# Attention with a pooled query, then a gated feed-forward: gates that take two heads on 128 partitions, a row tile per head into one PSUM bank

## The chip, the cores and the metric

The kernel runs on one core of a Trainium2 chip. The metric is device time in microseconds (us) of the whole kernel. Next to the time stands one profiled execution, whose trace gives every instruction's start, duration and what ended the engine's idle time. The kernel works in fp16 and fp32 and needs fp32 rows at the end.

## The reference, cut to what matters

Eight batches of eight heads, 1152 positions, 64 elements a head. Queries are averaged in pairs (576 rows), attend to 1152 keys, and the heads side by side (4608 rows of 512) go through a product of two gates and two more matrices.

```python
def _attn_ref(q, k, v):
    q_pool = q.reshape(B, H, S // 2, 2, D).mean(axis=3)
    scores = scale * np.matmul(q_pool, k.transpose(0, 1, 3, 2))
    attn = np.exp(scores - np.max(scores, axis=-1, keepdims=True))
    attn = attn / (np.sum(attn, axis=-1, keepdims=True) + 1e-09)
    return np.matmul(attn, v)

def _moe_ref(x, w1, w2, w3, w_out):      # x: 4608 x 512, dff = 1024
    a = x @ w1
    b = x @ w2
    h = a * b @ w3
    return h @ w_out
```

## The kernel before, in words

**Attention.** Work goes by pairs of heads: 32 pairs P, four to a batch. A head has 64 elements, so TensorE is used as two row tiles of 64 partitions that work beside each other; tile u holds head u of the pair. `scores` (L316) forms blocks of 512 columns of both heads into one of two double banks `psc`, and one exponential on ScalarE (`expo`, L322) of 128x1024 follows each: 324 of them, 10.125 a pair. They go into a ring `er`. When a pair's scores are through, `attend` (L339, L348) multiplies the probabilities with the values, 36 products of 65 columns for each head and 18 for the last 64 query rows of both; these products use the full array. `normalize` divides by the row sums on VectorE (L377 to L391) into `xn`, and a DMA on SyncE's queue transposes it to `xT` (L385). The last 64 query rows of each head of a batch (rems) are collected for four batches.

**Feed-forward.** w3 and w_out are multiplied once into T16 (`w3_transpose`, tiles w3t and pT, L513 to L538), so that what is left per batch is: gates `pg` (L580), a = x w1 and b = x w2, their product `gT` on VectorE (L571, after a copy `asb` of a, L558, or L555 on ScalarE after the last scores), and rows `pp` (L612) with T16, scaled into `osb` (L598, L602) and stored by SyncE. Before, `xn` of one head at a time is transposed, so even 128-row chunks of queries lie on partitions 0 to 63 and odd ones on 64 to 127: row tile 0 takes 256 tokens, row tile 1 the 256 others, over eight heads. Each tile fills a bank of its own with a and b (2 x 256 columns), with 16 products. Tile 1 needs the weights of every head on partitions 64 to 127 too and tile 0 on 0 to 63; so `swap_halves` (L445 to L452) makes a second copy of w1 and w2 with the halves swapped: 16 full-array products with a permutation, and 12 VectorE and 4 ScalarE copies. `cross` (L406) does the same for the remainders with DMAs.

**Two tiles in one bank.** Rows and T16 products sum over both tiles into one bank. There tile 0 does its eight products, VectorE reads an element of the bank (`handed`, L491), and only then does tile 1 add its eight.

**The order.** The schedule is by hand. A loop over the exponentials (L796 to L861) keeps a clock for each row tile, an estimate of VectorE's and ScalarE's progress, and four spare banks (`spare`, `take`, `give`). Scores come as soon as the exponential two before is estimated done (`due`); probability products come at the places in BEHIND and APART (J: both heads together; a digit: so many exponentials apart); in between, `step` emits the next product from two queues of feed-forward work, one for each tile, if its inputs and a bank are estimated ready. Tile 0 may lead tile 1 by LEAD. `add_batch` puts a batch's gates and rows into the queues. After the last exponential (`tail`) two more banks are given to them and ScalarE takes the copies of a and the scaling. The constants T_..., COLD, LANDS, STAGE, PREP, early and V_COPIED are that planner's.

**Loads.** GpSimd issues the loads of keys, queries, values and weights in the order of ORDER; from pair 7 on keys and queries are transposed by DMAs on SyncE's queue (L173, L180), before that by TensorE (`prep_pe`, tile t). The first queries are loaded to 64 partitions and added in pairs by VectorE (L233), transposed by TensorE (tq) and copied (L242).

Of the kernel before, what the change touches and what calls it, by code (L numbers as in the profile page):

```python
# [15 lines left out]
NJ = 9  # L16
# [8 lines left out]
def kernel(  # L25
# [21 lines left out]
    T_SC, T_ACT, T_EXP, T_SEM, T_PV, LEAD = 0.225, 0.93, 1.05, 0.25, (1.78, 1.4), 3.79  # L47
    COLD = 9.0
# [9 lines left out]
    xT = const.tile([128, H, 2, 512], FP16)  # L58
    w1sb = const.tile([128, 2, NC, dff], FP16)
    w2sb = const.tile([128, 2, NC, dff], FP16)  # L60
    T16 = const.tile([128, NF, dm], FP16)
    wosb = const.tile([128, NF, dm], FP16)
    xR0 = const.tile([128, 3, H // 2, 2, 2, 64], FP16)
    xR = [xR0, wosb.rearrange("p a b -> p (a b)")[:, 0:48 * D].rearrange(
        "p (o c k u r) -> p o c k u r", o=3, c=H // 2, k=2, u=2)]
# [3 lines left out]

    ident = const.tile([128, 128], FP16)  # L70
    swap = const.tile([128, 128], FP16)
    seen = const.tile([1, 2], FP16)
    handed = const.tile([1, 1], FP32)
# [69 lines left out]
    def pool_q(P, eng=None):  # L143

        pp, o = P // 2, 64 * (P % 2)
        if P % 2 == 0:
            qps[pp] = ab.tile([128, NJ, 2, D], FP16, tag="qp", bufs=2, name="qp")
        r = slice(o, o + 64)
        src = qst[pp][r].rearrange("p u (c two) d -> p u c two d", two=2)
        (eng or nc.vector).tensor_tensor(  # L150
            out=qps[pp][r].rearrange("p c u d -> p u c d"),
            in0=src[:, :, :, 0, :], in1=src[:, :, :, 1, :], op=ALU.add)
# [67 lines left out]
    def prep_first():  # L220
# [3 lines left out]
        qp = qps[0] = ab.tile([128, NJ, 2, D], FP16, tag="qp", bufs=2, name="qp")  # L224
        src = q0.rearrange("p u (c two) d -> p u c two d", two=2)
# [5 lines left out]
        for cs in parts:  # L231
            r = slice(cs[0], cs[-1] + 1)
            nc.vector.tensor_tensor(  # L233
                out=qp[0:64, r].rearrange("p c u d -> p u c d"),
                in0=src[:, :, r, 0, :], in1=src[:, :, r, 1, :], op=ALU.add)
        for h, cs in enumerate(parts):
            for c in cs:
                o = 64 * (c - cs[0])
                nc.tensor.transpose(tq[:, h, o:o + 64],
                                    qp[0:64, c].rearrange("p u d -> p (u d)"),  # L240
                                    ident[0:64, 0:64])
# [85 lines left out]
    def attend(P, us, js=range(NJ)):  # L327
# [35 lines left out]
        if 0 in us and b % 2 == 1:  # L363
            nc.sync.dma_start_transpose(
                out=xR[b // 4][:, 1, hp, (b // 2) % 2].rearrange("p u r -> p (u r)"),
                in_=rems[:, hp].rearrange("p s d -> p (s d)"))
        if 0 in us and hp == 3:
            landed = vec + (8.0 if b < 2 else 6.5)
            ended.append((b, [landed]))
            if b % 2 == 1:  # L370
                crossing.append((b, landed + (6.0 if b % 4 == 1 else 0.0)))

    def normalize(P, u, po, n, at):
# [5 lines left out]
        xn = ab.tile([128, 4, D], FP16, tag="xn", bufs=4, name="xn")  # L379
        nc.vector.tensor_tensor(  # L380
            out=xn, in0=acc[:, 0:4, 0:D],
            in1=rz[:, 0:4].to_broadcast([128, 4, D]), op=ALU.mult)
        k = (b // 2) % 2
        o = 256 * (b % 2)
        nc.sync.dma_start_transpose(  # L385
            out=xT[:, 2 * hp + u, k, o:o + 256].rearrange("p (i r) -> p i r", r=128),
            in_=xn.rearrange("p i d -> p (i d)"))
        vector(5, at)
        vector(256, at)
        if n == 5:  # L390
            nc.vector.tensor_tensor(  # L391
                out=rems[:, hp, b % 2, :], in0=acc[:, 4, 0:D],
                in1=rz[:, 4].to_broadcast([128, D]), op=ALU.mult)
            vector(64, at)
        return vec

    ended, kq_done, crossing = [], {}, []
    crossed = [[1e9], [1e9]]

    def cross():  # L400

        b, _ = crossing.pop(0)
        x = xR[b // 4]
        k = (b // 2) % 2
        for h in range(2):
            nc.sync.dma_start(out=x[64 * h:64 * h + 64, 2 - 2 * h, :, k],  # L406
                              in_=x[64 - 64 * h:128 - 64 * h, 1, :, k])
        if k == 1:
            crossed[b // 4][0] = max(clock) + 6.0
# [12 lines left out]
    def load_part(h, dst, src):  # L422
        cols = slice(512 * h, 512 * h + 512)
        nc.gpsimd.dma_start(out=dst[:, 0, :, cols],
                            in_=src.rearrange("(c p) f -> p c f", p=128)[:, :, cols])
        swaps[h].extend((dst, c, cols) for c in range(NC))
# [6 lines left out]

    swaps = ([], [])
    copied = [[1e9], [1e9]]

    def swap_halves():

        half = 0 if swaps[0] else 1
        dst, c, cols = swaps[half].pop(0)
        n = take()
        t = bank("sw", n)
        nc.tensor.matmul(t, swap, dst[:, 0, c, cols], start=True, stop=True)  # L445
        clock[:] = [max(clock) + 0.22] * 2
        if c % 3 == 1:
            nc.scalar.copy(out=dst[:, 1, c, cols], in_=t)
            done = exp_done[-1] = max(exp_done[-1], clock[0] + T_SEM) + 0.6
        else:  # L450
            nc.vector.tensor_copy(out=dst[:, 1, c, cols], in_=t)
            done = vector(512, clock[0])  # L452
        give(n, done)
        if not swaps[half]:
            copied[half][0] = done + T_SEM

    def swap_due():
        half = 0 if swaps[0] else 1
        free = 3 if prep[0] or prep[1] else 2
        if not swaps[half]:  # L460
            return False
        landed = LANDS[("f" if swaps[half][0][0] is w1sb else "g") + str(half)] + T_SEM
        return max(clock) > max(WEIGHTS[half], landed) and len(spare) >= free and (
            spare[0][0] < min(clock))
# [3 lines left out]
    class Block:  # L468
# [3 lines left out]
        def __init__(self, pre, n_products, tiles, then, dt=FP32):  # L472
            self.pre, self.n_products, self.tiles, self.then = pre, n_products, tiles, then
            self.dt, self.n, self.handed = dt, None, 1e9

# [5 lines left out]
        def product(self, n, h, emit):  # L481
# [3 lines left out]
            end = n == self.n_products - 1  # L485
# [4 lines left out]
            elif end:  # L490
                nc.vector.tensor_copy(out=handed, in_=self.t[0:1, 0:1])  # L491
                self.handed = vector(1, clock[h]) + T_SEM
# [5 lines left out]
    def add(queue, block, cost, ready, emit):  # L498


        for h in block.tiles:
            for n in range(block.n_products):
                queue[h].append((block, n, cost, ready(n) if callable(ready) else ready, emit))

    def w3_transpose(c):
# [4 lines left out]
        landed = LANDS["wo"]  # L510

        def out(t, at, h):
# [4 lines left out]
            if left[0] == 0:  # L517
                ready[0] = max(done + T_SEM, landed)
# [21 lines left out]
        add(ffn, Block("pT", NF, (0, 1), copy), 0.216, [ready], product)  # L540

    def unit(x, places, ready, split=False, final=False):

        gT = {}
        gdone = [[[1e9] for _ in range(NF)] for _ in range(2)]
        n = 256

        def gate(ft, h, both=False):  # L550
            def mul(t, at):
                asb = ffp.tile([128, n], FP32, tag="asb", bufs=3, name="asb")
                b, a = t[:, n:2 * n], asb
                if tail:
                    nc.scalar.copy(out=a, in_=t[:, 0:n])  # L555
                    at += 0.4
                else:
                    nc.vector.tensor_copy(out=a, in_=t[:, 0:n])  # L558
                    vector(n, at)
                if h not in gT:  # L560
                    if split:
                        g = ffp.tile([128, NF, 128], FP16, tag="row", bufs=7, name="gT")
                        gT[h] = g.rearrange("p a f -> p (a f)").rearrange(
                            "p (a f) -> p a f", f=n)
                    else:
                        gT[h] = ffp.tile([128, NF, n], FP16, tag="g", bufs=4, name="gT")
                g = gT[h][:, ft % 4 if split else ft, 0:n]
                if not split:
# [4 lines left out]
                gdone[h][ft][0] = done + T_SEM  # L573
                return done
            fs = slice(ft * 128, ft * 128 + 128)

            def emit(t, s, i, start, stop):
                w, m = divmod(i, H)
                o = s.start // 64
                nc.tensor.matmul(t[:, n * w:n * w + n], (w1sb, w2sb)[w][s, (m + o) % 2, m // 2, fs],  # L580
                                 x(o, s, m),
                                 start=start, stop=stop, skip_group_check=True)
            if both:
                queue = [], []
                add(queue, Block("pg", H, (0, 1), mul), 0.0025 + n / 2400,
                    [ready, copied[2 * ft // NF]],
                    lambda t, s, i, start, stop: emit(t, s, i + H * (s.start > 0), start, stop))
                for q, add_ in zip(ffn, queue):
                    q[-NF:-NF] = add_
                return  # L590
            add(ffn, Block("pg", 2 * H, (h,), mul), 0.0025 + n / 2400,
                [ready, copied[2 * ft // NF]], emit)

        def rows(h, o, places):
# [11 lines left out]
            cs = slice(o, o + 128)  # L606

            def g(s, i):
                return gT[i // 4][s, i % 4, cs] if split else gT[h][s, i, cs]
# [4 lines left out]
            if final:  # L614
                last.append((emit, store, places, lambda i: g(slice(0, 128), i)))
            else:
                add(ffn, Block("pp", NF, (0, 1), store), 0.216,
                    lambda i: [gdone[i // 4 if split else h][i]], emit)

        yield gate  # L620
        for h, o, to in places:
            rows(h, o, to)

    def add_batch(b, ready):

        k, o, end = (b // 2) % 2, 256 * (b % 2), b == B - 1
# [272 lines left out]
```

## Time and profile before

| what | value |
|---|---|
| runs | 413.22, 416.35, 416.85 us; median 416.35 |
| the profiled execution: own time, span of the trace | 410.37 us, 408.6 us |
| granted TensorE clock, mean | 0.996 |
| instructions in the span | 16883 |
| first scores, first gate | 8.97 us, 72.0 us |
| last product of TensorE ends | 404.7 us |
| LDWEIGHTS with w1 and w2 | 2 x 1152, mean 94 ns |
| transposes xT<-xn on SyncE's queue | 64, median 5.4 us to landing, about 1.2 us to issue |

The profile page gives busy time by engine, a picture in 40 slices, the chain of work that ended last, the costliest groups of instructions (line, engine, operation, tiles, shapes, count, busy us, mean ns, idle time before and what ended it) and DMA issues. A busy TensorE is not one at its peak: its products are pipelined, a 512-column product of a row tile has a duration of 376 ns and the next one on that tile starts sooner. So prices of products are read from their starts. PE is TensorE, PEld its weight loads, DVE VectorE, ACT ScalarE, POOL GpSimd, SP SyncE.

### The profile page before, as it was taken

Reading aid. Unit: us, or ns where it says so; the run is one execution under the profiler, and the core shown is the slowest. Engines: PE = TensorE matmul, PEld = TensorE weight load, DVE = VectorE, ACT = ScalarE, POOL = GpSimd, SP = SyncE. Lnnn points to the kernel's source line nnn. Section 1 sums busy time; section 2 is a strip of 40 time slices with the busy share of each in tenths; the row PEclk is TensorE's granted clock in tenths of the full one; section 3 lists DMA queues with packets and bytes.
Section 4 is the critical chain, followed back from the end, with each engine's and each line's share of the span. In section 5 each row is a group of like instructions: output and inputs, shape, how many; then the busy total and the mean of one; then the engine's idle time right before and its main releaser. Section 6 shows DMA issues by size and latency. Waiting matters only on the chain.

```text
span 408.6 us, 16883 instructions
## 1 busy us (share of the span) xinstructions
PE 392.5 (96%) x7356; PEld 316.5 (77%) x7356; DVE 213.8 (52%) x570; ACT 323.8 (79%) x369; POOL 241.1 (59%) x283
## 2 busy tenths in 40 slices
PE   2799999999999999999999999999999999999996
PEld 1377666868878977897789886799778878998884
DVE  2436775566445644664456654367346644652431
ACT  2979988889889798889988799789889788834432
POOL 6244246596987878779959787687978611000000
PEclk9989999999999999999999999999999999999999
DMA  8999999999999999999999999999999933103004
GB/s 181 210 206 203 177 194 192 147 146 143 165 187 205 126 128 171 189 159 161 192 183 158 131 146 131 189 204 173 118 211 206 118 81 116 29 18 117 3 28 129
DMA packets 121834, 60.99 MB, mean 149 GB/s; under 512 B 71456, under 2 KB 114976, under 8 KB 121760
## 3 DMA queue, kind: packets, MB, share of 16 engines
q0 software_dynamic: 47552, 32.98, 65.7%
q1 hardware_dynamic: 73776, 26.61, 43.2%
q8 instruction: 57, 0.93, 1.0%
q10 hardware_dynamic: 432, 0.33, 0.3%
q14 instruction: 17, 0.14, 0.1%
HBM read 67.11 MB, written 9.44 MB: 187 GB/s over the span
## 4 chain that ended last, share of the span: by engine, by line
PE 90%; DMA 6%; ACT 1%; DVE 1%; issue 1%; SPq 0%
PE pg L580 30%; PE psc L316 19%; PE po L339 18%; PE pp L612 15%; DMA qT<-qp 4%; PE pT L538 3%; PE po L348 3%; ACT er L322 1%; DMA er<-in_q_dram 1%; PE sw L445 1%; PE t L284 1%; PE w3t L522 1%; PE pp L689 0%; DVE w3T L513 0%; DVE kT L278 0%
## 5 line engine op out<-in xcount | busy, mean ns | idle before, releaser
L322 ACT ACTIVATE er<-psc 128x1024 f16<-128x1024 f32 x324 | 303.5, 1046 | 46.5 <-PE psc L316 46.2
L316 PE MATMUL psc<-qT,kT 64*128 64x512 f16 (+7 forms) x1152 | 130.8, 289 | 4.0 <-ACT er L322 3.1
L580 PE MATMUL pg<-xT,w2sb 64*128 64x256 f16 x1024 | 124.5, 269 | 0.8 <-issue 0.8
L580 PE MATMUL pg<-xT,w1sb 64*128 64x256 f16 x1024 | 123.3, 269 | 0.0
L580 PEld LDWEIGHTS <-w2sb 64*128 64x128 f16 x1152 | 93.6, 94 | 8.0 <-issue 1.4
L580 PEld LDWEIGHTS <-w1sb 64*128 64x128 f16 x1152 | 93.1, 94 | 7.7
L612 PE MATMUL pp<-T,gT 64*128 64x512 f16 (+1 forms) x552 | 93.9, 376 | 0.0
L316 PEld LDWEIGHTS <-kT 64*128 64x128 f16 x1152 | 63.8, 95 | 29.0 <-issue 14.1
L339 PEld LDWEIGHTS <-er 128*128 128x128 f16 x2304 | 73.8, 98 | 11.2 <-issue 9.7
L339 PE MATMUL po<-vt,er 128*128 128x65 f16 x2304 | 80.0, 194 | 0.1
L571 DVE TENSOR_TENSOR gT<-pg,asb 128x256 f16<-128x256 f32 x144 | 64.1, 445 | 20.0 <-ACT asb L555 15.0
L558 DVE COPY asb<-pg 128x256 f32<-128x256 f32 x116 | 49.0, 422 | 33.0 <-PE pg L580 32.2
L150 POOL TENSOR_TENSOR qp<-qst 64x1152 f16<-64x1152 f16 x25 | 59.3, 2373 | 2.0 <-DMA qst<-in_q_dram 1.2
L377 DVE RECIPROCAL rz<-po 128x4 f32<-128x4 f32 x64 | 12.1, 189 | 78.8 <-PE po L348 40.9
L612 PEld LDWEIGHTS <-gT 64*128 64x128 f16 (+1 forms) x552 | 39.3, 94 | 13.1 <-issue 0.4
L112 POOL DMA_DIRECT2D kst<-in_k_dram x46 | 33.0, 718 | 4.5 <-issue 4.1
L112 POOL DMA_DIRECT2D vst<-in_v_dram x46 | 33.6, 734 | 0.0
L159 POOL COPY vt<-vst 128x1152 f16<-128x1152 f16 x28 | 32.2, 1154 | 0.6
L185 POOL COPY seen<-kT 1x1 f16<-1x1 f16 x24 | 4.3, 179 | 47.5 <-DMA kT<-kc 47.5
L165 POOL COPY kc<-kst 128x1152 f16<-128x1152 f16 x25 | 29.0, 1161 | 3.2 <-DMA kT<-kc 3.2
L112 POOL DMA_DIRECT2D qst<-in_q_dram x46 | 28.8, 635 | 1.8 <-DMA w2sb<-in_moe_w_dram 1.8
L380 DVE TENSOR_TENSOR xn<-po,rz 128x256 f16<-128x256 f32 x64 | 27.2, 424 | 2.2
(68 smaller groups left out, 252.6 us busy)
## 6 DMA issues: line engine op xcount, KB each, us to landing
out_dram<-osb SPq DMA_DIRECT2D x32, 256.0 KB, 4.5
kst<-in_k_dram POOLq DMA_DIRECT2D x46, 144.0 KB, 4.9
qst<-in_q_dram POOLq DMA_DIRECT2D x46, 144.0 KB, 6.1
vst<-in_v_dram POOLq DMA_DIRECT2D x46, 144.0 KB, 5.6
vst<-in_v_dram POOLq DMA_DIRECT2D x9, 288.0 KB, 15.9
kst<-in_k_dram POOLq DMA_DIRECT2D x8, 288.0 KB, 15.7
qst<-in_q_dram POOLq DMA_DIRECT2D x8, 288.0 KB, 15.8
w3h<-in_moe_w_dram POOLq DMA_DIRECT2D x4, 512.0 KB, 14.6
```

Of the source, the lines that this page charges most:

```text
L112: nc.gpsimd.dma_start(out=dst[:, u], in_=src[:, u], max_dma_last_dim=RUN)
L150: (eng or nc.vector).tensor_tensor(out=qps[pp][r].rearrange("p c u d -> p u c d"), in0=src[:, :, :, 0, :], in1=src[:, :, :, 1, :], op=ALU.add)
L159: (eng or nc.vector).tensor_copy(out=vts[P % 4][:, :, :, 0:D], in_=vst.pop(P))
L165: nc.gpsimd.tensor_copy(out=kcp[P].rearrange("p j u d -> p u j d"), in_=kst.pop(P))
L316: nc.tensor.matmul(t[:, u, o:o + ln], kT[P][s, j, :], qv[s, f0:f0 + ln], start=True, stop=True)
L322: nc.scalar.activation(out=er[:, :, r:r + CH], in_=psc.pop(c), func=AF.Exp, bias=0.0, scale=SCALE)
L339: nc.tensor.matmul(po[:, VW * i:VW * i + D + 1], er[:, u, r:r + 128], vts[P % 4][:, u, j, 0:D + 1], start=(j == 0 and i == 0), stop=(j == ...
L380: nc.vector.tensor_tensor(out=xn, in0=acc[:, 0:4, 0:D], in1=rz[:, 0:4].to_broadcast([128, 4, D]), op=ALU.mult)
L558: nc.vector.tensor_copy(out=a, in_=t[:, 0:n])
L571: nc.vector.tensor_mul(out=g, in0=b, in1=a)
L580: nc.tensor.matmul(t[:, n * w:n * w + n], (w1sb, w2sb)[w][s, (m + o) % 2, m // 2, fs], x(o, s, m), start=start, stop=stop, skip_group_chec ...
L612: nc.tensor.matmul(t, g(s, i), T16[s, i, :], start=start, stop=stop, skip_group_check=True)
```

## The change

Both heads of a pair are normalised into one tile `xn` and transposed together, so xT has two heads on 128 partitions and four chunks of 128 partitions make the 512 elements. Row tile 0 takes the even heads, tile 1 the odd heads, with the weights as they are loaded. A gate product takes 512 tokens; a and b each have a bank, and in it tile 0 does four products, VectorE reads it (`handed`, now two elements, 255 and 256), and tile 1 adds its four. The swapped weights, their products and copies, and the crossing DMAs are gone. The remainders of four batches are 256 tokens, with a and b in one bank, handed over in the same way. The remainder rows are normalised in two operations of 64 partitions. At the end one block of rows has some of tile 1's products moved to tile 0 (T16m, gTm, MOVED). w_out is loaded in two halves and later; the first queries are loaded and added on 128 partitions; and the planner's constants and places have other values.

```diff
-    T_SC, ..., LEAD = 0.225, 0.93, 1.05, 0.25, (1.78, 1.4), 3.79
-    COLD = 9.0
+    T_SC, ..., LEAD = 0.225, 0.93, 1.05, 0.25, (1.78, 1.4), 4.15
+    COLD = 11.0
+    MOVED = 6
-    xT = const.tile([128, H, 2, 512], FP16)
-    w1sb = const.tile([128, 2, NC, dff], FP16)
+    xT = const.tile([128, NC, 4, 512], FP16)
+    w1sb = const.tile([128, NC, dff], FP16)
...
-            nc.vector.tensor_tensor(
-                out=qp[0:64, r].rearrange("p c u d -> p u c d"),
-                in0=src[:, :, r, 0, :], in1=src[:, :, r, 1, :], op=ALU.add)
+            nc.vector.tensor_tensor(
+                out=qp0[:, r], in0=src[:, r, 0, :], in1=src[:, r, 1, :], op=ALU.add)
...
-        nc.sync.dma_start_transpose(
-            out=xT[:, 2 * hp + u, k, o:o + 256].rearrange("p (i r) -> p i r", r=128),
-            in_=xn.rearrange("p i d -> p (i d)"))
+        if u == 0:
+            nc.sync.dma_start_transpose(
+                out=xT[:, hp, b % 4].rearrange("p (i r) -> p i r", r=128),
+                in_=xns.pop(P).rearrange("p i u d -> p (i u d)"))
...
-    def cross():
-    def swap_halves():
-        nc.tensor.matmul(t, swap, dst[:, 0, c, cols], start=True, stop=True)
...
-                nc.vector.tensor_copy(out=handed, in_=self.t[0:1, 0:1])
+                nc.vector.tensor_copy(out=handed, in_=self.t[0:1, 255:257])
...
-                nc.tensor.matmul(t[:, n * w:n * w + n], (w1sb, w2sb)[w][s, (m + o) % 2, m // 2, fs],
-                                 x(o, s, m),
-                                 start=start, stop=stop, skip_group_check=True)
-            add(ffn, Block("pg", 2 * H, (h,), mul), 0.0025 + n / 2400,
-                [ready, copied[2 * ft // NF]], emit)
+            def one(w):
+                def then(t, at):
+                    return mul(t, at) if other else copy(t, at)
+                def emit(t, s, m, start, stop):
+                    nc.tensor.matmul(t, (w1sb, w2sb)[w][s, m, fs], x(s, m), start=start,
+                                     stop=stop, skip_group_check=True)
+                add(ffn, Block("pg", NC, TILES[w], then), 0.216, [ready, landed], emit)
+            if n == 512:
+                one(0)
+                one(1)
+            else:
+                add(ffn, Block("pg", 2 * NC, TILES[ft % 2], both), 0.109, [ready, landed], emit)
...
+    TILES = ((0, 1), (0, 1))
+        if b == 1:
+            nc.sync.dma_start(out=T16m, in_=T16[64:128, 0:MOVED])
...
-    ORDER = ("v0 k1 q1 w0 wo k2 q2 v1 w1 k3 q3 v2 w2 k4 q4 v3 w3 k5 q5 v4 "
-             "f0 g0 k6 q6 v5 k7 q7 f1 g1 v6 k8 q8 v7").split()
+    ORDER = ("k1 q1 k2 w0 w1 q2 k3 v0 wa v1 wb v2 q3 w2 k4 q4 v3 w3 k5 q5 "
+             "v4 f0 g0 k6 q6 v5 k7 q7 f1 g1 v6 k8 q8 v7").split()
...
-    early = list(zip((7, 7, 17, 18, 31, 41, 41, 43), range(8)))
+    early = list(zip((4, 5, 6, 6, 16, 25, 33, 40), range(8)))
...
-    BEHIND = "22422222333442422221223242212432"
-    APART = "33344434J2J4JJJ221JJ36JJ3J3JJ4JJ"
+    BEHIND = "22211122212224242421222424342442"
+    APART = "3J2235226564232426516JJ515J32215"
```

274 lines of the change are left out of this document (115 added, 159 removed).

## The prediction, made before the changed kernel ran

> **What bounds the kernel now.** I read the page's busy shares, the chain that ended last and the costliest groups; then the core's windows, cut at the starts of exponentials 1, 21, 41, 61, 81, 101 and 321 of 324; then the timeline and chain at places where one kind of product follows itself.
>
> ```profile
> PE 392.5 (96%) x7356; PEld 316.5 (77%) x7356; DVE 213.8 (52%) x570; ACT 323.8 (79%) x369; POOL 241.1 (59%) x283
> PE pg L580 30%; PE psc L316 19%; PE po L339 18%; PE pp L612 15%; DMA qT<-qp 4%; PE pT L538 3%; PE po L348 3%; ACT er L322 1%; DMA er<-in_q_dram 1%; PE sw L445 1%; PE t L284 1%; PE w3t L522 1%; PE pp L689 0%; DVE w3T L513 0%; DVE kT L278 0%
> L322 ACT ACTIVATE er<-psc 128x1024 f16<-128x1024 f32 x324 | 303.5, 1046 | 46.5 <-PE psc L316 46.2
> ```
>
> TensorE carries 90% of the chain. ScalarE's exponentials are the second bound: busy 303.5 us, and its 46.5 us of idle time end at scores, so it waits for TensorE and not the reverse.
>
> ```profile
> core 0: us, PE busy (x) PEld busy (x) DVE busy (x) ACT busy (x) POOL busy (x), PEclk, DMA share, GB/s
> 9.60:30.80 21.20, 18.25 (x287) 11.78 (x289) 8.85 (x24) 18.70 (x21) 7.35 (x12) 0.92 1.18 208
> 30.80:51.00 20.20, 20.03 (x401) 14.40 (x398) 14.18 (x37) 18.85 (x21) 6.98 (x10) 1.00 1.23 190
> 51.00:73.50 22.50, 22.49 (x423) 15.03 (x423) 14.34 (x37) 19.98 (x24) 12.63 (x15) 1.00 1.23 191
> 73.50:95.90 22.40, 21.96 (x416) 17.06 (x414) 14.28 (x35) 19.93 (x24) 18.27 (x19) 1.00 1.46 141
> 95.90:118.70 22.80, 21.97 (x407) 16.94 (x404) 10.71 (x31) 18.80 (x21) 19.52 (x23) 1.00 1.37 157
> 118.70:356.30 237.60, 237.54 (x4678) 198.70 (x4676) 129.25 (x348) 205.31 (x222) 169.71 (x192) 1.00 1.23 155
> 356.30:408.60 52.30, 48.41 (x753) 41.48 (x747) 19.49 (x53) 19.98 (x43) 0.00 (x0) 1.00 0.18 59
> ```
>
> The run has three stages: A, exponentials 1 to 100 (9.6 to 118.7: 109.1 us); B, 101 to 320 (237.6 us); C, from 321 on (52.3 us), where gates and rows stand alone and the last 3.9 us are the output's way. Prices come from these rows:
>
> ```profile
> 11.99 0.61 PE L316 MATMUL psc<-qT,kT 64*128 64x192 f16 x4 [0.69 <-ACT er L322]
> 12.91 0.61 PE L316 MATMUL psc<-qT,kT 64*128 64x256 f16 x4 [0.30 <-ACT er L322]
> ...
> 201.13 0.38 PE L612 MATMUL pp<-T,gT 64*128 64x512 f16 x1
> ...
> 201.35 0.38 PE L612 MATMUL pp<-T,gT 64*128 64x512 f16 x1
> ...
> 399.02 0.27 PE L580 MATMUL pg<-wosb,w2sb 64*128 64x256 f16 x1
> ...
> 399.13 0.27 PE L580 MATMUL pg<-wosb,w2sb 64*128 64x256 f16 x1
> ```
>
> ```profile
> 185.98 1.20 PE po L339 x36
> ...
> 189.04 0.41 PE po L348 x18
> ```
>
> Where scores wait only for ScalarE they start 0.917 us apart: that is the exponentials' pace. On one row tile, 512-column rows start 0.215 us apart and 256-column gates 0.11; the other tile works beside it. Probability products take 33 ns and 23 ns.
>
> **A rule from these rows.** TensorE takes its products in order, and scores wait for the exponential two before. So I went through the built order of both kernels, summed the products between the scores of one exponential and the next (columns x 0.42 ns per row tile, the later tile counts, and the prices above), and let two neighbouring gaps together last no less than 2 x 0.917 us. For before this gives A 104.9, B 239.5, C 48.4 + 3.9. Measured: 109.1, 237.6, 52.3. B is met within 1%; A has 4.2 us more than the rule, 1.9 of it in the first 20 exponentials and about 1.3 in the two windows from 51.0 to 95.9, where the swap's copies lie.
>
> **The change, part by part.**
>
> Gates: 2304 products of 256 columns become 1024 of 512 and 256 of 256; the columns are the same 589,824. By the rows two of 256 take 2 x 0.11 = 0.22 and one of 512 0.215, equal within their reading, so I take 0 (bounds 0 and 1024 x 5 ns / 2 tiles = -2.6). 1024 weight loads go, which overlap in any case. The Trainium skill ("TensorE: Matmul & The Clock Gate", Back-to-back issue gap) puts a warm product at its columns / 2.4 plus 2.5 ns; by that the halving would be worth 1024 x 2.5 / 2 = 1.3 us, inside these bounds.
>
> Swaps: 16 products and their 12 VectorE and 4 ScalarE copies go. The products are in the rule's A. ScalarE's copies (586 ns each) stand between exponentials; beyond the rule the windows from 51.0 to 95.9 hold 1.3 us, and I take that away (bounds 0 and 4 x 0.586 = 2.3).
>
> Order: in 512-column products on both tiles, A has 64 to 72 of gates and 26 to 24 of rows, no swap for 16; B 385.8 to 345 of gates and 182 to 172 of rows; C 126.2 to 159 and 80 to 92. So some 10 us of work move behind the last exponential. Sums of products: A 94.7 to 89.6, B 233.7 to 225.1, C 48.4 to 58.7. By the rule A falls 104.9 to 102.6 (-2.3), B 239.5 to 232.4 (-7.1: in B more gaps than before are shorter than the exponentials, so 8.6 us less work gives 7.1), and C grows by 10.3. The probability products stand in 59 runs for 50, since more pairs take their two heads apart; that is in the rule's prices.
>
> Start: the queries' second half is added on 128 partitions, 320 elements for 640. That add took 0.82 us and stands in the chain right behind its transfer; half is 0.41. I take -0.4 (bounds 0, if the transfer lands later, and -0.8, if transposes on two tiles gain as much again).
>
> VectorE: the 512-wide copies and products cost 691 ns (below) for two of 422 and two of 445; 144 hand-overs at 146 ns add 21.0 us, 32 more remainder products at 214 ns add 6.8 at most; 12 swap copies take away 8.2. In sum it stays near 214 us and is no bound. DMA queues: 64 transposes of x become 32 of double length, the eight crossing copies go, one copy of T16 comes; on SP's queue that is fewer issues (64 x 1.2 us) ahead of the keys' and queries' transposes. A batch's last x lands later by the longer transpose, between 0 and 6.7 - 5.4 = 1.3 us (keys against x, median landing), hidden by the previous batch's rows. Cost 0.
>
> New waits: with a row tile per head in one bank, tile 1 starts only when VectorE has read the bank behind tile 0, and each bank now comes free by a 691 ns operation.
>
> ```profile
> L602 DVE TENSOR_SCALAR osb<-pp 128x512 f32<-128x512 f32 x26 | 18.0, 691 | 12.3 <-PE pp L612 11.5 <-DMA wosb<-rems 0.7
> L491 DVE COPY handed<-pp 1x1 f32<-1x1 f32 x34 | 5.0, 146 | 21.9 <-PE pp L612 21.3 <-PE psc L316 0.6
> ```
>
> A VectorE operation that sat waiting starts 0.414 us after the start of a 512-column product, 0.2 after its streaming, and TensorE answers 0.05 after a release (scores after an exponential). A bank's turn thus needs 0.20 + 0.69 + 0.05 = 0.94 us, a hand-over 0.40. In the built order the least work between the last product in a bank and the next use was 1.92 us before; now 13 of 77 such places have less than 0.94, mostly 0.85, and 19 more less than 1.1. Hand-overs have 0.64 or more in 105 of 106 places. If VectorE is free: 12 x 0.09 = 1.1 us; I take +1.0. Low end 0, if the gap holds idle time anyway; high end: VectorE is 54% busy in B (129.25 of 237.6), and one operation ahead costs up to 0.69, so some 32 x 0.54 x 0.69 = 12. Behind a stopped product all of TensorE's queue waits, the scores too. The Trainium skill ("TensorEngine Tiling (Array Packing)", Gotcha 1) says that two row tiles can't be in one bank at once and software must order them; before shows such an order for its rows, with 42 hand-overs and no wait of TensorE for one over 150 ns, so the trace agrees and shows it cheap at this rate.
>
> Sum on the span: start -0.4, A -2.3 - 1.3, B -7.1, C +10.3, waits +1.0, gates 0: +0.2. Span 408.6 to 408.8, and with the 1.8 us around it 410.6 for 410.37. The median shown, 416.35, is 1.46% above that execution; scaled, 416.5. It is no change.
>
> **Rivals.**
> 1. Faster: stage A loses all that it has beyond the rule. The windows from 51.0 on had 22.5 us and more per 20 exponentials against 21.6 to 21.9 by the rule; if the swaps caused that and also held the first windows back, the remaining 2.9 go. With gates at -2.6 and no bank wait (-1.0): 0.2 - 6.5 = -6.3, 410.0. For it: the swaps are the only full-width products there. Against: 1.9 of it is the first 20 exponentials, with no swap.
> 2. Slower: the bank's turn. Place: the 32 places above, in B; price up to +12 for the +1 taken: 11 more, 427.7; half of it, 422. It decides (over 1%, +4.1 us) when a place costs 0.16 us on average. For it: 13 places below what the rows need. Against: the slack in such places counts products alone, and the pace of exponentials leaves gaps there.
> 3. The first query transpose by DMA (pair 7) comes too late.
>
> ```profile
> 84.91 0.20 PE L316 MATMUL psc<-qT,kT 64*128 64x64 f16 x2 [0.43 <-DMA qT<-qp]
> ```
>
> It was issued at 67.67 and took 17.2 us in the chain, with the DMA share at 1.46. If the 70 exponentials ahead run 3.6 us sooner and it lands when it did, A's gain is given back: +3.6, 420.2. Against: its issue moves with the exponentials.
> 4. The change doesn't do what it says: both tiles of a bank serialise. The order sets tile 1 of one block beside tile 0 of the next, as before's rows do at 0.215 a tile; I give it nothing.
>
> **How the numbers follow.** A measurement of this kernel tells about 1% from no change (the three runs spread 0.9%). Forecast 0.41, rival 1 0.30, rival 2 0.20, rival 3 0.09. Faster by over 1%: rival 1 and a little of the forecast's edge, 0.31. Slower by over 1%: rival 2 and some of rival 3, 0.24. Within 1%: 0.45. The range goes from rival 1 less its start bound (-0.4, and the copies' -1.0: 408.5) to past half of rival 2 (423). The likeliest case's own range is 413 to 420.
>
> **What would show it.** Right: no sw rows; gates' 512-column rows 0.215 apart on a tile; exponential 321 starts some 10 us earlier, near 346, and 62 to 63 us follow it; ScalarE's idle time for scores falls. Wrong: TensorE waits for gT, asb, osb or handed of more than some 5 us in all (rival 2); windows of 20 exponentials in A below the rule's 21 (rival 1); a wait for qT<-qp of more than 1 us (rival 3); or gaps in B that are no longer met by the rule.

## The result, and the profile after

| | before | after |
|---|---|---|
| median of 19 runs each, us | 411.93 (408.54 to 416.85) | 418.33 (416.99 to 420.67) |
| ratio, 95% interval | | 1.0167 [1.0142, 1.0193] |
| span of the profiled execution, us | 408.6 | 416.5 |
| mean granted clock (recorded from 17.1 and from 29.1 us on) | 0.996 | 0.998 |

The change makes the kernel slower by 1.7%. (The 416.35 us that the forecast started from was the median of three runs; over 19 it is 411.93, and the profiled execution of 410.37 lies near that.) Some executions of a kernel are over 1.5% longer than its fastest; the ratios leave them out, and in experiments 6 and 8 the profiled execution is one of them.

The same cuts as in the prediction, at the starts of exponentials 1, 21, 41, 61, 81, 101 and 321; columns as there:

```profile
core 0: us, PE busy (x) PEld busy (x) DVE busy (x) ACT busy (x) POOL busy (x), PEclk, DMA share, GB/s
7.70:37.50 29.80, 16.55 (x290) 10.40 (x291) 11.14 (x28) 18.72 (x21) 13.13 (x19) 1.00 1.17 204
37.50:58.90 21.40, 20.46 (x422) 15.08 (x422) 12.83 (x36) 18.65 (x21) 7.81 (x13) 1.00 1.20 201
58.90:81.30 22.40, 21.31 (x404) 15.30 (x404) 14.51 (x37) 19.08 (x21) 15.90 (x15) 1.00 1.26 173
81.30:102.60 21.30, 21.30 (x353) 14.11 (x350) 13.02 (x37) 18.84 (x22) 15.74 (x17) 1.00 1.05 131
102.60:123.50 20.90, 20.46 (x332) 12.97 (x329) 8.87 (x26) 18.82 (x22) 11.23 (x14) 1.00 1.07 167
123.50:353.60 230.10, 230.10 (x3866) 161.40 (x3862) 123.99 (x356) 206.14 (x221) 173.30 (x197) 1.00 1.14 153
353.60:416.50 62.90, 58.35 (x652) 37.67 (x648) 24.37 (x84) 21.91 (x39) 0.00 (x0) 0.99 0.17 57
```

The trace of the changed kernel has no record of the clock before 29.14 us, so the 1.00 of the first row says nothing about the time up to there (experiment 1 comes back to it).

| stretch | before | after | change | forecast |
|---|---|---|---|---|
| start (to the first exponential) | 9.6 | 7.7 | -1.9 | -0.4 |
| A: exponentials 1 to 20 | 21.2 | 29.8 | +8.6 | A in all: -3.6 |
| A: exponentials 21 to 100 | 87.9 | 86.0 | -1.9 | |
| B: 101 to 320 | 237.6 | 230.1 | -7.5 | -7.1, and +1.0 for bank waits |
| C: from 321 on | 52.3 | 62.9 | +10.6 | +10.3 |
| span | 408.6 | 416.5 | +7.9 | +0.2 |

The surprise is one row: the first 20 exponentials take 29.8 us. In that window TensorE is busy for 16.55 us, VectorE for 11.14, ScalarE for 18.72: no engine is the bound, something waits. The waits name it, first TensorE's (what waited, for what, us in all, times, longest), then VectorE's from 0 to 60 us:

```profile
engine line waited for: us in total, times, longest us
PE t L281 <- DVE kc L207: 10.7, 1, 10.7
PE tq L238 <- DVE er L232: 4.5, 1, 4.5
PE psc L313 <- ACT er L319: 3.0, 7, 0.7
...
PE pp L574 <- DVE handed L444: 0.2, 1, 0.2
```

```profile
DVE vt L159 <- DMA vst<-in_v_dram: 13.3, 1, 13.3
```

Read one after the other: TensorE waits 10.7 us for `kc`, the rearranged keys of pair 1, which VectorE makes; but VectorE stands in front of another instruction, the copy of the *values* of pair 0. The timeline has it in order (start, duration, instruction, idle time before and what ended it):

```profile
9.64 0.75 POOL L109 DMA_DIRECT2D vst<-in_v_dram  x1
...
22.36 0.46 DVE L159 COPY vt<-vst 128x1152 f16<-128x1152 f16 x1 [13.33 <-DMA vst<-in_v_dram]
...
22.74 0.45 DVE L207 COPY kc<-kst 128x1152 f16<-128x1152 f16 x1
...
23.25 0.29 PE L281 MATMUL t<-ident,kc 64*128 64x64 f16 x4 [10.72 <-DVE kc L207]
...
24.00 2.85 ACT L319 ACTIVATE er<-psc 128x1024 f16<-128x1024 f32 x3 [10.30 <-PE psc L313]
```

and before, the same load and the same two copies:

```profile
3.74 0.84 POOL L109 DMA_DIRECT2D vst<-in_v_dram  x1
...
10.85 0.45 DVE L159 COPY vt<-vst 128x1152 f16<-128x1152 f16 x1
...
11.42 0.46 DVE L207 COPY kc<-kst 128x1152 f16<-128x1152 f16 x1
```

The new ORDER puts the load of v0 behind k1, q1, k2, w0, w1, q2 and k3: eighth where it was first. It is issued at 9.64 for 3.74 and lands at 22.3 for 10.0: 5.9 us of later issue, and 12.7 us on the way for 6.2, with seven loads ahead of it. The copy that needs it is the last line of `prep_rest`, ahead of pair 1's keys on VectorE, which takes its instructions in order. So a load that nobody needs until pair 0's values are multiplied holds the keys of pair 1. TensorE is in order too: it has the transposes of these keys ahead of pair 0's own last scores, whose keys and queries had been ready since 9.0 us (the seventh exponential starts at 24.00), and so ScalarE stands for 10.3 us. The rest of the profile is close to the forecast: one wait for a hand-over is listed, of 0.2 us, and exponential 321 starts at 353.6 with 62.9 us behind it.

### The profile page after: what moved, and what is told of

It reads as the page before. It is cut to its first block, busy times and chain, and to the rows that moved or that the text cites. A ratio compares the mean times of both kernels' runs of the same rounds, so it can differ in the third digit from the quotient of the medians.

```text
span 416.5 us, 14905 instructions
## 1 busy us (share of the span) xinstructions
PE 390.6 (94%) x6325; PEld 268.2 (64%) x6325; DVE 210.9 (51%) x611; ACT 324.4 (78%) x361; POOL 240.9 (58%) x282
## 4 chain that ended last, share of the span: by engine, by line
PE 90%; DMA 4%; ACT 2%; POOL 1%; DVE 1%; issue 1%; DVEq 0%
PE pg L539 28%; PE po L336 18%; PE psc L313 18%; PE pp L574 14%; PE pg L549 3%; PE po L345 3%; DMA vst<-in_v_dram 3%; PE pT L490 3%; ACT er L319 2%; DMA T<-in_k_dram 1%; PE t L281 1%; POOL kst L109 1%; DVE kc L207 0%; PE pp L660 0%; POOL w3h L400 0%
## 5 line engine op out<-in xcount | busy, mean ns | idle before, releaser
L313 PEld LDWEIGHTS <-kT 64*128 64x128 f16 x1152 | 66.0, 94 | 42.6 <-issue 15.5
L574 PE MATMUL pp<-T,gT 64*128 64x512 f16 (+1 forms) x546 | 91.5, 376 | 0.4 <-DVE handed L444 0.2
L539 PE MATMUL pg<-xT,w1sb 64*128 64x512 f16 x512 | 90.3, 376 | 0.0
L539 PE MATMUL pg<-xT,w2sb 64*128 64x512 f16 x512 | 88.3, 376 | 0.0
L524 DVE TENSOR_TENSOR gT<-pg,asb 128x512 f16<-128x512 f32 (+1 forms) x80 | 53.8, 673 | 13.6 <-PE pg L539 8.7
L539 PEld LDWEIGHTS <-w2sb 64*128 64x128 f16 x512 | 33.8, 94 | 19.0 <-DVE rems L388 2.2
L539 PEld LDWEIGHTS <-w1sb 64*128 64x128 f16 x512 | 33.7, 94 | 19.0 <-DVE rems L388 1.5
L512 DVE COPY asb<-pg 128x512 f32<-128x512 f32 (+1 forms) x57 | 36.8, 646 | 7.9 <-PE pg L539 6.8
L444 DVE COPY handed<-pg 1x2 f32<-1x2 f32 x144 | 20.7, 143 | 34.0 <-PE pg L539 31.5
L185 POOL COPY seen<-kT 1x1 f16<-1x1 f16 x24 | 4.3, 179 | 52.3 <-DMA kT<-kc 52.3
L510 ACT COPY asb<-pg 128x512 f32<-128x512 f32 (+1 forms) x23 | 11.8, 511 | 23.2 <-PE pg L539 17.3
## 6 DMA issues: line engine op xcount, KB each, us to landing
w3h<-in_moe_w_dram POOLq DMA_DIRECT2D x4, 512.0 KB, 12.7
```

Source lines behind the costliest of these rows:

```text
L313: nc.tensor.matmul(t[:, u, o:o + ln], kT[P][s, j, :], qv[s, f0:f0 + ln], start=True, stop=True)
L444: nc.vector.tensor_copy(out=handed, in_=self.t[0:1, 255:257])
L512: nc.vector.tensor_copy(out=asb, in_=t[:, 0:n])
L524: nc.vector.tensor_mul(out=g, in0=b, in1=a)
L539: nc.tensor.matmul(t, (w1sb, w2sb)[w][s, m, fs], x(s, m), start=start, stop=stop, skip_group_check=True)
L574: nc.tensor.matmul(t, g(s, i), T16[s, i, :], start=start, stop=stop, skip_group_check=True)
```

## The experiments

All times are medians in us, with the ratio to the kernel before in the same job and its 95% interval. "This kernel" is the changed one. Stage spans are those of the profiled execution, cut as above, one for each kernel. The runs of the kernel before alone go from 408.54 to 416.85 us, so a difference of 1 to 3 us between the stages of two kernels can be spread.

| kernel | us | ratio | start | first 20 | A | B | C |
|---|---|---|---|---|---|---|---|
| before | 411.93 | | 9.6 | 21.2 | 109.1 | 237.6 | 52.3 |
| after | 418.33 | 1.0167 [1.0142, 1.0193] | 7.7 | 29.8 | 115.8 | 230.1 | 62.9 |
| 1 after, v0 first | 417.44 | 1.0132 [1.0080, 1.0184] | 7.6 | 21.4 | 113.8 | 233.1 | 62.9 |
| 2 after, copy of v0 later | 418.13 | 1.0125 [1.0055, 1.0195] | 7.5 | 26.2 | 116.0 | 230.2 | 62.9 |
| 3 before, v0 late | 421.94 | 1.0232 [1.0170, 1.0295] | 9.8 | 27.8 | 115.0 | 238.8 | 54.8 |
| 4 before, no swap | 416.22 | 1.0095 [1.0054, 1.0136] | 9.3 | 19.8 | 107.3 | 242.0 | 52.5 |
| 5 after, hand-overs twice | 422.60 | 1.0264 [1.0213, 1.0316] | 7.8 | 29.9 | 118.3 | 231.8 | 63.1 |
| 6 as 1, pair 7 by TensorE | 412.56 | 1.0013 [0.9964, 1.0062] | 7.7 | 21.5 | 116.7 | 230.2 | 62.5 |
| 7 before, pair 7 by TensorE | 419.08 | 1.0193 [1.0137, 1.0249] | 9.8 | 19.7 | 110.3 | 241.9 | 55.0 |
| 8 as 6, v0 third | 413.93 | 0.9965 [0.9894, 1.0036] | 7.8 | 22.0 | 116.0 | 230.2 | 62.5 |
| 9 as 8, pair 7 prepared by GpSimd | 418.00 | 1.0120 [1.0066, 1.0173] | 7.8 | 20.5 | 106.7 | 236.3 | 66.6 |
| 10 before, first queries on 128 partitions | 413.38 | 1.0015 [0.9978, 1.0052] | 7.8 | 22.6 | 110.7 | 240.5 | 52.3 |

The theory after the result: the late load of v0 is the whole loss, by VectorE's queue. The rivals: the hand-overs inside banks; the loss of the swaps or another part of the change; or a kernel that has another wait ready as soon as this one goes.

**1. This kernel, v0 first again.**

```diff
-    ORDER = ("k1 q1 k2 w0 w1 q2 k3 v0 wa v1 wb v2 q3 w2 k4 q4 v3 w3 k5 q5 "
+    ORDER = ("v0 k1 q1 k2 w0 w1 q2 k3 wa v1 wb v2 q3 w2 k4 q4 v3 w3 k5 q5 "
```

> The changed kernel with pair 0's values moved from the eighth to the first place of the load order. Theory (VectorE's in-order queue stands 13.3 us behind the copy of these values, and the keys' copy of pair 1 stands behind it): TensorE's wait of 10.7 us for kc goes, the first 20 exponentials take 20 to 22 us for 29.8, the span is 405 to 408, which is 1% below to the same as before. Rival (loads as a whole are too slow for the earlier start, or the rest of the change costs as much): a wait of 7 us or more stays at the first keys, span 413 or more.

The stall is gone, as the theory says (first 20: 21.4 us for 29.8), and the time hardly moves: 1.0132. (The traced execution is the longest of its six, which go from 413.23 to 419.19 us.) Some 8 us won at the start are lost again further on; the span is 417.4, where 405 to 408 was expected. Exponentials 61 to 80 take 27.9 us for 21.2, and the timeline, the chain of waits and three windows from 84 to 96 us show why (B, longer by 3.0 us, has a gap of 1.9 as well that the profile gives to "issue"):

```profile
87.30 0.24 PE L313 MATMUL psc<-qT,kT 64*128 64x64 f16 x2 [3.78 <-DMA qT<-qp]
```

```profile
72.35 14.91 DMA qT<-qp
```

```profile
core 0: us, PE busy (x) PEld busy (x) DVE busy (x) ACT busy (x) POOL busy (x), PEclk, DMA share, GB/s
84.00:88.00 4.00, 0.70 (x6) 0.35 (x7) 0.00 (x1) 0.39 (x2) 3.91 (x3) 0.79 1.67 105
88.00:92.00 4.00, 4.00 (x29) 1.74 (x26) 1.50 (x4) 2.20 (x3) 0.54 (x1) 0.50 1.35 184
92.00:96.00 4.00, 4.00 (x97) 3.48 (x96) 0.99 (x4) 2.48 (x4) 3.84 (x6) 0.85 1.44 164
```

This is the prediction's rival 3: pair 7's queries, the first that a DMA transposes, were issued at 72.35, took 14.9 us, and are late by 3.8 us. The wait costs more than its length, since the trace has a granted clock of 0.50 from 86.34 to 93.16, 5.9 us of it behind the wait: 29 products in 88 to 92, 97 in the 4 us after. The Trainium skill ("TensorE: Matmul & The Clock Gate", Part 1: The HAM clock gate) says that an idle window of some 3.4 us lowers the clock to half and a busy one brings it back; this wait and the 0.50 behind it agree. The 10.7 us wait at the start of the changed kernel is no exception, though its row shows 1.00: the record of the clock begins behind it, at 29.14 us, and the scores in between are slow.

```profile
25.08 0.61 PE L313 MATMUL psc<-qT,kT 64*128 64x512 f16 x2
```

The same pair of products takes 0.39 us at 34.94. Before shows the same step, from 0.61 us at 16.57 to 0.39 at 17.49, where its record begins with the full clock at 17.09. So the changed kernel's clock was still at half for some 6 us after the stall.

What the stall at the start had hidden was a second wait. In the changed kernel pair 7's transpose was issued at 79.66, 7.3 us later than here, most of the 8.7 by which exponential 61 was later; but it took 5.3 us for 14.9, and so was in time. Why it took less, no run shows.

**2. This kernel, the copy of v0 moved behind the first scores.**

```diff
-        copy_v(0)
...
+        if c == 9:
+            copy_v(0)
```

> The changed kernel with its own load order, but VectorE's copy of pair 0's values stands nine exponentials later in its queue, behind the keys and queries of pair 1. Theory (the queue, not the late data alone): the wait for pair 1's keys goes; what is left is the wait for the values, which land near 22.4 us while the first probability products would be due near 19 to 20: 2 to 5 us, span 408 to 412. If only the late landing counts: span 415 to 417 as it was.

TensorE's wait for `kc` goes, but the copy only stands in another place of the same queue. VectorE's waits from 0 to 60 us, and TensorE's:

```profile
DVE vt L159 <- DMA vst<-in_v_dram: 7.5, 1, 7.5
```

```profile
PE w3t L473 <- DVE w3T L464: 5.8, 1, 5.8
```

With a ratio of 1.0125 it recovers little: the first 20 take 26.2 us for 29.8, and exponentials 41 to 60 lose the same again (26.0 for 22.4, with a gap of 2.5 us that the profile gives to "issue"). The expectation, a span of 408 to 412, was missed at 416.6. What is late is the load; where its copy stands only decides which product pays for it.

**3. The kernel before, v0 seventh.** One part of the change alone:

```diff
-    ORDER = ("v0 k1 q1 w0 wo k2 q2 v1 w1 k3 q3 v2 w2 k4 q4 v3 w3 k5 q5 v4 "
+    ORDER = ("k1 q1 w0 wo k2 q2 v0 v1 w1 k3 q3 v2 w2 k4 q4 v3 w3 k5 q5 v4 "
```

> The kernel before with the one part alone: pair 0's values moved from the first to the seventh place of its load order. Theory: VectorE stands behind their copy, TensorE waits 6 to 11 us for the first keys' copies, span 414 to 420. Rival (it is the swap-free gates and their hand-overs that cost): within 2 us of before.

TensorE's waits, and VectorE's from 0 to 60 us:

```profile
PE t L284 <- DVE kc L207: 8.0, 1, 8.0
```

```profile
DVE vt L159 <- DMA vst<-in_v_dram: 11.5, 1, 11.5
```

The same two waits, and the first 20 go from 21.2 to 27.8. The kernel before becomes slower by 2.3%, as much as by the whole change or more. So the place of this load alone is enough for the loss, with no gate, bank or swap touched. (C is 2.5 longer too: the planner, with other landing times, leaves 11 more gate products of 512 columns on both tiles behind exponential 320.)

**4. The kernel before, no swap.** The swap's products and copies are left out, and row tile 1 reads the unswapped weights, so the gates of the output are computed with the wrong halves of w1 and w2.

```diff
-        swaps[h].extend((dst, c, cols) for c in range(NC))
+        copied[h][0] = max(WEIGHTS[h], LANDS[("f" if dst is w1sb else "g") + str(h)] + T_SEM)
...
-                nc.tensor.matmul(t[:, n * w:n * w + n], (w1sb, w2sb)[w][s, (m + o) % 2, m // 2, fs],
+                nc.tensor.matmul(t[:, n * w:n * w + n], (w1sb, w2sb)[w][s, 0, m // 2, fs],
```

> The kernel before without the 16 swap products and their 16 copies; row tile 1 reads the weights as they are loaded, so its gates are of the wrong half: that part of the computation is changed. By the rule of the prediction the swaps are worth 16 x 0.287 = 4.6 us of products and 1.3 us of copies in stage A where it is bound by products, span 403 to 406. Rival (they stand in gaps that the exponentials leave anyway): within 1 us of before.

Both expectations are missed: the span is 411.1, and the end comes later by 0.95%. A falls by 1.8 us, but 1.4 of that is in the first 20 exponentials, where no swap stands (the first is at 53.7 us). Of the windows that hold the swaps in before, exponentials 41 to 60 take 0.9 us less and 61 to 80 take 1.6 more, with a wait of 2.0 for pair 7's queries; 81 to 100, which hold none, take 1.1 less. So this does not price the swaps; what it shows is that some of the work taken away in A comes back at once as a wait for pair 7. B grows by 4.4 us, and why is not shown (TensorE's waits list 1.4 and 1.1 us of "issue", where the trace names no releaser).

**5. This kernel, each hand-over made twice.**

```diff
                 nc.vector.tensor_copy(out=handed, in_=self.t[0:1, 255:257])
+                nc.vector.tensor_copy(out=handed, in_=self.t[0:1, 255:257])
```

> The changed kernel with every hand-over's VectorE read made twice, so 186 of them take 0.29 us for 0.14. Theory (hand-overs and bank turns have room): exponentials 101 to 320 stay within 2 us of 230.1, and what follows within 2 us of 62.9. Rival (they hold TensorE): each of some 180 costs up to 0.14 us more, 10 us or more in the two stages together.

All 186 hand-overs have a second copy of 146 ns in front of tile 1: 30 in A, the others in B and C. B grows by 1.7 us, C by 0.2, and TensorE waits 0.4 us in all for a hand-over, in one wait:

```profile
PE pp L575 <- DVE handed L445: 0.4, 1, 0.4
```

If each had stood on the path, 156 x 0.146 = 22.8 us would have come in B and C, for 1.9. So single hand-overs have room there, and the 1.7% is not theirs. A grows by 2.5 us, where its 30 can give 4.4 at most; the waits do not say whether they did (one VectorE addition of queries there took 1.94 us for 0.74).

**6. As 1, and pair 7 transposed by TensorE** (prepared by VectorE in the place of GpSimd):

```diff
-    NPE = 7
+    NPE = 8
...
-        + [(4.6, 7, prep_pool), (4.8, 9, load), (5.6, 8, prep_pool), (5.75, 10, load), (6.45, 9, prep_pool)]
+        + [(4.8, 9, load), (5.6, 8, prep_pool), (5.75, 10, load), (6.45, 9, prep_pool)]
...
-        [(5.1, 7, turn_k), (5.4, 7, turn_q), (6.1, 8, turn_k), (6.35, 8, turn_q), (6.6, 8, more)]
+        [(6.1, 8, turn_k), (6.35, 8, turn_q), (6.6, 8, more)]
```

> The changed kernel with pair 0's values first in the load order, and with the keys and queries of pair 7 also transposed by TensorE, as those of pairs 1 to 6, instead of by DMA. Theory (with the stall at the start gone, exponentials run into the late landing of pair 7's transposed queries; they waited 3.8 us and the granted clock fell to 0.50, so exponentials 61 to 80 took 27.9 us for 21.2): these 20 take 21 to 23 us, span 407 to 411. Rival a: the wait moves to pair 8, the next by DMA, and exponentials 81 to 100 take 25 us or more, span 413 or more. Rival b: the loss lies in stage B or C, which stay as they are.

1.0013 [0.9964, 1.0062]: with both the load's place and pair 7's DMA taken away, the change makes no difference that can be told, as the prediction's sum has it (with the reservation of experiment 7 on this edit's own price). The profiled execution shows one more wait in A, exponentials 41 to 60 at 29.1 us, because one VectorE addition took 5.51 us. Its timeline, VectorE's row and GpSimd's beside it:

```profile
69.91 5.51 DVE L150 TENSOR_TENSOR qp<-qst 64x1152 f16<-64x1152 f16 x1
```

```profile
70.25 1.16 POOL L159 COPY vt<-vst 128x1152 f16<-128x1152 f16 x1
71.34 1.16 POOL L165 COPY kc<-kst 128x1152 f16<-128x1152 f16 x1
72.45 2.34 POOL L150 TENSOR_TENSOR qp<-qst 64x1152 f16<-64x1152 f16 x1
```

The same kind of addition took 0.76 us in the profile before, at 12.88 us, and pair 7's own takes 0.76 in experiment 7. The traced execution took 418.89 us, where the median is 412.56; whether the addition is as long in the others is not known. Here it ends 0.6 us behind GpSimd's last. The Trainium skill ("SBUF — State Buffer", SBUF: two separate sides) says that a VectorE operation with two SBUF inputs and a GpSimd one that reads SBUF lock each other out of a shared port for a whole instruction. The trace agrees that the loser stands still, for three operations in a row: 1.16 + 1.16 + 2.34 = 4.7 of the 5.5 us. By that section the one that starts first wins, and here VectorE's record starts first, 69.91 against 70.25; in experiment 8 both start at 70.26. The spans of GpSimd's records are rough, so this is no proof of an exception.

**7. The kernel before, pair 7 transposed by TensorE:** the same edit as in 6, in the kernel before.

> The kernel before with pair 7 transposed by TensorE. Theory: its wait for pair 7's queries was 0.4 us, and 27 more transposes and three VectorE copies come, so the span stays within 2 us of 408.6; a gain of 3 us or more would mean that before too was held by that transfer.

It is 1.9% slower, where the expectation was 2 us at most: C +2.7, B +4.3, and 2.8 and 2.4 us of waits of TensorE that the profile puts down to "issue" alone. So the edit of 6 is no gain in itself. C has 11 more gate products of 512 columns on both tiles, some 2.4 us at 0.215 each. Why B is longer was not found; exponentials 281 to 300 hold 3.0 us of it, with the gap of 2.4.

**8. As 6, with v0 third** (k1 and q1 first):

```diff
-    ORDER = ("v0 k1 q1 k2 w0 w1 q2 k3 wa v1 wb v2 q3 w2 k4 q4 v3 w3 k5 q5 "
+    ORDER = ("k1 q1 v0 k2 w0 w1 q2 k3 wa v1 wb v2 q3 w2 k4 q4 v3 w3 k5 q5 "
```

> As the run with values first and pair 7 on TensorE, but the values stand third in the load order, behind pair 1's keys and queries. Theory: they land about 1.5 MB of loads earlier than in the changed kernel, near 12 to 14 us, and VectorE waits 1 to 4 us for them but TensorE under 2; span 407 to 412. Rival: a wait of 3 us or more at the first keys, span 412 or more.

0.9965 [0.9894, 1.0036], from two of its four runs. The place first or third makes no difference that can be told, and the version is no gain over the kernel before that can be told either. The profiled execution has the same long addition, 5.17 us.

**9. As 8, pair 7 prepared by GpSimd,** so that VectorE has no such addition:

```diff
+    def pool_for_pe(P):
+        prep_pool(P)
+        kcs[P] = kcp.pop(P)
...
-        + [(4.6, 7, prep_pool), (4.8, 9, load), (5.6, 8, prep_pool), (5.75, 10, load), (6.45, 9, prep_pool)]
+        + [(4.6, 7, pool_for_pe), (4.8, 9, load), (5.6, 8, prep_pool), (5.75, 10, load), (6.45, 9, prep_pool)]
```

> The changed kernel with pair 0's values third in the load order; pair 7's keys and queries are made ready by GpSimd as in the changed kernel and transposed by TensorE instead of by DMA, so that VectorE adds no queries while GpSimd is at work (that one add took 5.2 to 5.5 us for 0.75 in the two runs before, with GpSimd busy beside it). Theory: no wait over 3 us after the start, 20 exponentials take 21 to 23 us everywhere in stage A, span 405 to 409, 0.5 to 1.5% below before. Rival (stage A is bound by loads as a whole): a wait of 3 us or more comes up elsewhere before exponential 100, span 411 or more.

Stage A is clean for once: 106.7 us, every 20 exponentials in 20.5 to 22.7, and exponential 101 starts at 114.5 us where this kernel has 123.5. And then it is given back. TensorE's waits and the chain of waits from 85 to 118 us:

```profile
PE psc L319 <- DMA qT<-qp: 4.4, 3, 2.7
```

```profile
93.73 10.11 DMA qst<-in_q_dram
...
104.39 10.69 DMA qst<-in_q_dram
```

Exponentials 101 to 120 take 26.1 us; the loads of the queries themselves are 10.1 and 10.7 us on the way, with this window inside the first:

```profile
95.00:100.00 5.00, 4.94 (x116) 3.74 (x115) 1.98 (x6) 3.78 (x5) 4.27 (x4) 1.00 1.66 127
```

and C is 66.6, as the planner has left more work behind: 12 more products of gates and rows, counted as above. The span is 417.3 where 405 to 409 was expected. In this kernel an attention stage that runs ahead meets its loads and transposes behind exponential 100, as it met pair 7's in experiment 1.

**10. The kernel before, first queries loaded and added on 128 partitions:** the start of the change alone.

```diff
-                out=qp[0:64, r].rearrange("p c u d -> p u c d"),
-                in0=src[:, :, r, 0, :], in1=src[:, :, r, 1, :], op=ALU.add)
+                out=qp0[:, r], in0=src[:, r, 0, :], in1=src[:, r, 1, :], op=ALU.add)
...
+    nc.sync.dma_start(out=q0[:, 0:8], in_=src_q[:, 0:8])
+    nc.scalar.dma_start(out=k0[:, :, 0:3], in_=src_k[:, :, 0:3])
+    nc.sync.dma_start(out=q0[:, 8:18], in_=src_q[:, 8:18])
```

> The kernel before with the one part alone: the first queries loaded, added and transposed on 128 partitions. In the changed kernel the first exponential started at 7.7 us for 9.6. Theory (the two transfers are issued in 0.40 us each for 0.72 and land 1.6 us sooner, the adds take 0.49 for 0.82): first exponential at 7.5 to 8.2. Whether the end moves by as much is open, since pair 7's queries bound stage A: span 406 to 409. Rival (the change's other load order frees the transfer): first exponential at 9.2 or later.

The first exponential comes at 7.8 us for 9.6, the changed kernel's whole gain at the start, and the end does not move: 1.0015 [0.9978, 1.0052]. A is 1.6 longer, 1.4 of it in the first 20 exponentials; further on TensorE waits 1.3 us for pair 7's queries, and B is 2.9 longer, with 1.6 us of "issue" in it. With 1, 4 and 9 it is the fourth kernel in which microseconds won early are gone later.

## Why the prediction's number held by luck and its account did not: one moved load was not priced

**Forecast and result.** It gave no change at 416.5 us, the 410.37 of the profiled execution scaled by 1.0146 to a median of three runs. Measured are 418.33 and a ratio of 1.0167, which is clear of no change. That 416.5 lies near 418.33, and 418.33 inside 408.5 to 423, is luck: the median of three runs lay 4.4 us above that of 19, and the upper part of the range stood there for bank waits, which did not come. In the span it was +0.2 forecast against +7.9.

**The step that failed** is the one on queues: "DMA queues: ... Cost 0." It follows SP's queue and its transposes of x, and leaves GpSimd's out. The diff shows v0 going from first to eighth in ORDER, and the trace of before had all that was needed: loads stand some 0.7 us apart there, `vt<-vst` is copied at 10.85, and `kc` right behind it at 11.42, on one engine in order. Seven loads ahead at 0.6 to 0.8 us are 5 us of later issue alone, and two of the loads passed are weights; k2, with about as much ahead of it there, was issued at 7.49 and landed at 22.4. Experiment 3 puts that step's price at 1.0232 in the kernel before; in this kernel it is the 10.7 us wait, +8.6 in the first 20 exponentials. No rival had it: their waits were for banks and for pair 7. But the step is not the whole loss by itself. With v0 put back alone 1.0132 of 1.0167 stays (experiment 1), because rival 3, at a chance of 0.09, then comes true; only with both taken away is the loss gone (experiment 6, with the reservation made there).

**Start, -0.4; measured -1.9.** Right in sign, too small. The halved second add is 0.49 us for 0.82, but the transfers are ready sooner as well: the adds start at 4.03 and 5.43, and stood at 4.71 and 7.06 before. The bound of -0.8 held too little. Experiment 10 has the same -1.8 alone, and that it is worth nothing at the end.

**A, -2.3 and -1.3 for the swaps; measured -1.9 outside the first 20.** That is about half of the 3.6 forecast, and experiment 4 does not tell the swaps' share. The 1.9 us that the prediction found beyond its rule in the first 20 go with the clock of that one execution: its trace has it at 0.50 from 20.51 to 23.92, and they take 21.2 us, where experiments 4 and 7, whose edits come later, take 19.8 and 19.7 without such a fall. The reading behind the terms, that what is won in A reaches the end, is what the runs do not bear out: in experiments 1 and 9 it is lost at pair 7 or at the loads behind it, and in 4 and 10 there in part, in part in B.

**B, -7.1 and +1.0; measured -7.5.** The rule of the prediction gives B 232.4, and 230.1 were measured, within 1%. Nothing of the bank waits shows: no wait of TensorE for asb, osb or gT is in the list above 0.2 us. The low end, 0, was the right value.

**C, +10.3; measured +10.6.** 10 us of gates and rows moved behind the last exponential, as the built order said. Exponential 321 was forecast near 346, and starts at 353.6, late by the stall.

**Gates, 0.** B is met without a term for them; where gates stand alone in C, a 512-column gate product starts every 0.107 to 0.109 us over both tiles, 0.216 on one tile, as priced. The terms for the gates, the order of the work, the swaps and the hand-overs all come out within 2 us.

**Rival 2 (banks, +11)** is refuted by experiment 5 and by the waits. **Rival 3 (pair 7's queries)** did not occur in the changed kernel, where its DMA was issued 7.3 us later than in experiment 1 but took 5.3 us for 14.9, and came true in experiment 1, with 3.8 us and the clock's fall behind it: it decides what is left when v0 is put back. **Rival 1 (faster)** is not reached by any version: the best, experiment 8, is 0.9965 with an interval across 1.

**What stays open.** Single gaps of 1 to 3 us that the profile gives to "issue" differ from kernel to kernel (1.9 in experiment 1, 2.5 in 2, 2.8 and 2.4 in 7), and no run says what they wait for. In 3, 7 and 10, all versions of the kernel before, one of 1.5 to 2.4 us stands at 322 to 326 us, where the profile of before itself has none. The planner also writes a new order for each edit: 1, 2, 5, 6 and 8 have as many gates and rows in each stage as this kernel, and 10 as the kernel before, but in 3, 4, 7 and 9 it moved some from one stage to another, and part of their differences is its work.

## What to carry to other kernels

In a diff, follow every load that changes place to its first reader, and then ask what stands behind that reader on its engine: an in-order queue makes all of it as late as the load. A stall that is taken away is worth only what the next late thing allows, so look for that one (here a DMA with 15 us to land) before counting the gain. Work that is halved in number but not in columns is worth nothing where the columns are the price, and a hand-over inside a bank is nearly free where other products fill the gap.

## What the hardware showed that was not expected

- A TensorE wait of 3.8 us left 5.9 us at a granted clock of 0.50 behind it (experiment 1). Behind the 10.7 us wait in the changed kernel the clock's record is missing until 29.14 us and the windows print 1.00 for it; the durations of the scores, 0.61 us for 0.39, show the half clock all the same.
- A VectorE addition of 64x1152 fp16 took 5.51 us beside three GpSimd operations (experiment 6) and 0.76 us alone.
- A DMA transpose of queries took 14.9 us with a DMA share of up to 1.67 in its window (experiment 1), where the same one took 5.3 in the changed kernel; and plain loads of queries of 144 KB took 10.1 and 10.7 us (experiment 9), where their median over the changed kernel is 4.8.
- 156 more copies of 146 ns on VectorE, each in front of a product of TensorE, cost B and C 1.9 us together (experiment 5).
